# Attention with a position bias, a dense layer and top-2 experts on one core: an integer intermediate moved to PSUM, a 64-column subtraction moved to GpSimd, and another order for the last pair of experts

## The chip, the cores and the metric

The kernel runs on one core of a Trainium2 chip. The metric is the device time of one execution in microseconds, the median of three runs. The core has five engines with a queue of instructions each: TensorE (PE, and PEld for its weight loads), VectorE (DVE), ScalarE (ACT), GpSimd (POOL) and SyncE (SP), which here only issues DMAs. Every engine takes its own instructions in the order in which they stand in its queue.

## The reference

Three layers follow one another. B = 2, 8 heads, 576 positions, 64 numbers per head; 1152 rows of 512 numbers between the layers.

```python
scores = scale * q @ k^T + bias          # bias from a small MLP of |i - j|, one table per head
attn = softmax(scores)
x = (attn @ v)                           # (2, 8, 576, 64) -> (1152, 512)

h = x @ w_in                             # 512 -> 2048, weights given as float64
x = (h * sigmoid(h)) @ w_out             # 2048 -> 512

logits = x @ w_gate + log1p(exp(x @ w_noise)) * noise
top2, top2_w = ...                       # two of 8 experts for each row, softmax of their logits
for e in range(8):
    out[rows of e] += weight * (relu(x[rows of e] @ w1[e]) @ w2[e])
```

## The kernel before

**Two 16-bit parts.** TensorE multiplies float16. Every float32 operand is split into a high part, rounded to float16, and a low part, which is the rest; a product is then two or three matmuls. The split is an ACT copy to float16 and a subtraction on DVE or POOL.

**Attention** (`attention`, `att`). The 576 query rows are five chunks (four of 128 rows for each batch, one of 64 rows for both batches together), called a to e. For each chunk, head and batch there is one tile of 128 queries by 576 keys, 72 tiles in all. A tile's steps: scores on PE (lines 388 and 391), bias added and row maximum taken on DVE (431), a scalar (435), the exponential on ACT (436), its float16 copy `pr` on ACT (438), the low part of keys 0 to 511 on POOL (through the helper's line 117), and the low part of the last 64 keys on DVE (442). Then one DMA transposes `pr` (451, issued by SP), and PE multiplies by V (456, 457, 459). `xf` (467) ends four heads of a chunk.

**Bias waves** (`bias_wave`). For each chunk a table of the bias is made in 18 groups: a mask on DVE (`mk`, 337), 16 small matmuls into one PSUM tile `pb` (345, 346), one half taken out of it by DVE (359) and one by ACT (361), and their sum on POOL.

**Weight conversion** (`conv`). `w_in` and `w_out` arrive as float64 and are turned into float32 with integer operations, in 32 pieces of 128 by 512. DVE reads the high word and masks and shifts it (500), joins the sign (504) and the low word's top bits (505), all into the int32 tile `tt`, which lies in SBUF. ACT scales it in place (509) and writes the high part (510), POOL writes the low part (511). All 32 pieces go this way.

**PSUM.** Eight banks: the tag `gen` has three tiles of one bank, used in turn by `pb`, by `ph` of the dense layer and the experts, and by some smaller ones; `pq` has two tiles of two banks (scores, expert outputs), `av` one bank. A tile of a tag takes the place of the one allotted three earlier, and waits until that one has been read.

**Order.** Through the first two thirds bias waves, attention, conversion and dense layer are merged by a list of due times (`PLAN`, `merge`). A scheduler then sets the order in each engine's queue, so an edit in one place can move instructions in another.

**Experts** (`experts`). The eight experts go in four pairs g = 0 to 3, each expert with 320 slots for rows. `up(k, c0, n)` multiplies by w1 for n slots (lines 979 to 981, eight groups of 12 matmuls), with the activation on ACT (985) and the low part on DVE (986). `down(k, c0, col)` multiplies 128 slots by w2 (995 to 997, 24 matmuls). `down_last` does the remaining 64 slots of both experts together (1010). Each result is scaled on ACT (964) and added to the output by an indirect DMA that POOL issues (958); each of these waits for the one before.

```python
            yield from chain(up(0, 0, CAP), up(1, CAP, CAP))
        yield from down_last()
        if g > 0:
            yield from chain(down(0, 0, 0), down(1, 192, 1))
        yield from chain(down(0, 128, 2), down(1, 64, 3))
```

Of the kernel before, what the change touches and what calls it, by code (L numbers as in the profile page):

```python
# [23 lines left out]
CAP = 320  # L24
# [84 lines left out]
def body(ctx, tc, nc, A):  # L109
# [298 lines left out]
    def attention(c, xT):  # L408
# [3 lines left out]
        for hg in range(2):  # L412
# [5 lines left out]
            for h in range(4 * hg, 4 * hg + 4):  # L418
                bt = bias_load(c, h)
                if h % 4 == 1 and nxt is not None and nxt not in QT:  # L420
                    q_prep(*nxt)
                pqs = []
                for bi, b in enumerate(bs):
                    parts = [(0, 128, b)] if c < 4 else [(0, 64, 0), (64, 64, 1)]
                    if bi == 0 or c not in JQ:
                        qs = range(bi, nb if c in JQ else bi + 1)
                        scores(c, h, QT[c, hg], qs, pqs)
                    pq = pqs[bi]
                    z = at.tile([128, S], F32, name="z", tag="z", bufs=3)
                    st = at.tile([128, 4], F32, name="st", tag="st", bufs=4)  # L430
                    LAST["z", c, h, bi] = V.tensor_tensor_reduce(out=z, in0=pq, in1=bt, scale=1.0, scalar=NEG,  # L431
                                           op0=OP.add, op1=OP.max, accum_out=st[:, 1:2])
                    if h == 0 and c in ZX:
                        follow(LAST["z", c, h, bi], "xl")
                    V.tensor_scalar(st[:, 2:3], st[:, 1:2], -0.125, LN256, op0=OP.mult, op1=OP.add)  # L435
                    SC.activation(z, z, AF.Exp, bias=st[:, 2:3], scale=0.125, accum_out=sums[:, bi, h % 4:h % 4 + 1])  # L436
                    pr = at.tile([128, 2 * S], F16, name="pr", tag="pr", bufs=3)
                    SC.activation(pr[:, :S], z, AF.Copy)  # L438
                    if PLO:
                        V.tensor_sub(pr[:, 640:640 + PLO], z[:, :PLO], pr[:, :PLO])  # L440
                    STT(G, pr[:, 640 + PLO:1152], z[:, PLO:512], 1.0, pr[:, PLO:512])
                    V.tensor_sub(pr[:, 576:640], z[:, 512:], pr[:, 512:576])  # L442
                    pt = at.tile([128, 1152], F16, name="pt", tag="pt", bufs=3).rearrange("p (k q) -> p k q", k=9)
                    if c == ORDER[0] and h >= PTP:
                        for k0, k1 in ((0, 5), (5, 9)):
                            pp = gen("pp").bitcast(F16).rearrange("p (k q) -> p k q", q=128)
                            for k in range(k0, k1):
                                PE.transpose(pp[:, k - k0], pr[:, 128 * k:128 * k + 128], eye0)
                            SC.activation(pt[:, k0:k1], pp[:, :k1 - k0], AF.Copy)
                    else:  # L450
                        SP.dma_start_transpose(out=pt, in_=pr)
                    for p0, n, bb in parts:
                        o = av[p0:p0 + n, bi, h % 4, :]
                        for k in range(5):
                            lt = pt[:, k, p0:p0 + n]
                            mm(o, lt, VH[:, k, bb, h, :], start=(k == 0), stop=False)
                            mm(o, lt, VL[:, k, bb, h, :], start=False, stop=False)
                        for k in range(4):
                            mm(o, pt[:, 5 + k, p0:p0 + n], VH[:, k, bb, h, :], start=False, stop=(k == 3))
                    yield  # L460
# [25 lines left out]
    def conv(key, half, src):  # L486

        hi, lo = wtile(), wtile()
        WT[key, half] = (hi, lo)
        for pc in range(8):  # L490
            if pc % 3 in RG.get((key, half), ()):
                raw = m1.tile([128, 512], mybir.dt.int64, name="raw", tag="gt", bufs=NGT)
            else:
                raw = m1.tile([128, 512], mybir.dt.int64, name="raw", tag="raw", bufs=NRAW)
            with tc.issue_after(LAST[GATE].ins):
                SC.dma_start(raw, src(pc))
            v = raw.bitcast(I32).rearrange("p (n t) -> p n t", t=2)
            lw, hw = v[:, :, 0], v[:, :, 1]
            tt = m1.tile([128, 512], I32, name="tt", tag="yT", bufs=2)
            i = V.tensor_scalar(tt, hw, 0x07FFFFFF, 3, op0=OP.bitwise_and, op1=OP.logical_shift_left)  # L500
            if (key, half) in GC:
                follow(i, GC[key, half])
            LAST["tt", key, half, pc] = i
            V.scalar_tensor_tensor(tt, hw, -1073741824, tt, op0=OP.bitwise_and, op1=OP.bitwise_or)  # L504
            V.scalar_tensor_tensor(tt, lw, 29, tt, op0=OP.logical_shift_right, op1=OP.bitwise_or)  # L505
            f = tt.bitcast(F32)
            cs = slice(512 * pc, 512 * pc + 512)
            if pc in CP[key][half]:
                SC.activation(f, f, AF.Copy, scale=32.0)
                SC.activation(hi[:, cs], f, AF.Copy)  # L510
                G.tensor_sub(lo[:, cs], f, hi[:, cs])  # L511
            else:
                SC.activation(hi[:, cs], f, AF.Copy, scale=32.0)
                STT(V, lo[:, cs], f, 32.0, hi[:, cs])
            yield
# [117 lines left out]
    def chain(*gs):  # L633
        for g in gs:
            yield from g
# [331 lines left out]
    def experts(g):  # L967
# [3 lines left out]
        def up(k, c0, n):  # L971

            a_h, a_l = EW[2 * g + k, 0]
            for f in range(8):
                ph = gen("ph")[:, :n]
                for j in range(4):
                    cs = slice(1024 * j + 128 * f, 1024 * j + 128 * f + 128)
                    xh, xl = xg[:, j, c0:c0 + n], xg[:, 4 + j, c0:c0 + n]
                    mm(ph, a_h[:, cs], xh, start=(j == 0), stop=False)  # L979
                    mm(ph, a_h[:, cs], xl, start=False, stop=False)  # L980
                    mm(ph, a_l[:, cs], xh, start=False, stop=(j == 3))  # L981
                if (k, f) not in hts:
                    hts[k, f] = m2.tile([128, 2, CAP], F16, name="ht", tag="ht", bufs=20)
                ht = hts[k, f][:, :, c0 - CAP * k:c0 - CAP * k + n]
                SC.activation(ht[:, 0], ph, AF.Relu)  # L985
                V.scalar_tensor_tensor(ht[:, 1], ph, 0.0, ht[:, 0], op0=OP.max, op1=OP.subtract)  # L986
                yield
# [27 lines left out]

        if g == 0:
            yield from chain(up(0, 0, 128), up(1, 512, 128), down(0, 0, 0), down(1, 192, 1), up(0, 128, 192), up(1, 320, 192))
        else:
            yield from chain(up(0, 0, CAP), up(1, CAP, CAP))
        yield from down_last()  # L1020
# [113 lines left out]
```

## Time and profile before

| What | Value |
|---|---|
| median of 3 runs | 755.66 us (752.59 to 762.42) |
| the profiled execution, its own time | 758.37 us |
| its span in the trace | 756.6 us |
| busy over the span: PE, DVE, ACT, POOL | 606.9, 502.3, 377.9, 366.5 us |

The profile is one execution. "Busy" counts an instruction from its start to its end, with any time for which it is held up inside. "Idle before" is the time for which an engine had nothing running, put down to what it waited for. The span is the stretch from the first to the last instruction; 1.8 us of the execution lie around it.

### The profile page before, as it was taken

How to read it: one execution, taken by the hardware profiler on the slowest of the kernel's cores; microseconds unless marked ns; L12 is line 12 of the kernel's file. 1: busy time of each engine (PE TensorE's matmuls, PEld its weight loads, DVE VectorE, ACT ScalarE, POOL GpSimd, SP SyncE). 2: the span in 40 equal slices, each digit the busy share in tenths (PEclk: the TensorE clock that was granted, in tenths of full speed). 3: DMA queues.
4: the chain of work that ended last, by engine and by line, in shares of the span. 5: the costliest groups of instructions: out<-in, count | busy, mean ns of one | idle time of the engine just before them, and what ended most of it. 6: DMA issues, size and time to landing. Idle time of an engine off the chain costs nothing.

```text
span 756.6 us, 16562 instructions
## 1 busy us (share of the span) xinstructions
PE 606.9 (80%) x6371; PEld 402.6 (53%) x6371; DVE 502.3 (66%) x1093; ACT 377.9 (50%) x805; POOL 366.5 (48%) x366
## 2 busy tenths in 40 slices
PE   0565666578587878997999889979889899999992
PEld 0462344456344666565765664757665554655640
DVE  2999999999999699556952755656657642740200
ACT  2666467668644577345732644761355543541210
POOL 2686677687967687436761552303405114103022
PEclk9875557599788998998999999999999999999996
DMA  4547788778876699887996967764999959903123
GB/s 113 135 140 243 158 161 179 183 210 186 159 179 182 161 174 199 145 172 116 159 237 124 183 129 220 192 225 110 238 240 246 308 182 230 299 4 42 17 25 43
DMA packets 203143, 125.77 MB, mean 166 GB/s; under 512 B 153076, under 2 KB 175732, under 8 KB 203060
## 3 DMA queue, kind: packets, MB, share of 16 engines
q1 hardware_dynamic: 170868, 90.39, 52.2%
q10 hardware_dynamic: 27648, 24.32, 11.0%
q0 software_dynamic: 4544, 9.97, 7.1%
q8 instruction: 51, 0.84, 0.4%
q14 instruction: 32, 0.26, 0.1%
HBM read 74.83 MB, written 18.22 MB: 123 GB/s over the span
## 4 chain that ended last, share of the span: by engine, by line
PE 29%; DVE 29%; DMA 18%; issue 11%; ACT 4%; POOL 4%; SPq 3%; ACTq 1%; another core or an unknown queue 1%; DVEq 0%; POOLq 0%
DMA stg<-in_e 6%; DVE mk L337 4%; PE ph L979 3%; DVE z L431 3%; DMA pt<-pr 3%; PE ph L981 3%; DVE pr L442 3%; PE ph L980 3%; DVE tt L504 3%; DVE tt L505 3%; PE po L1010 3%; DVE tt L500 2%; PE po L996 2%; PE po L995 2%; PE po L997 2%
## 5 line engine op out<-in xcount | busy, mean ns | idle before, releaser
L117 POOL TENSOR_TENSOR pr<-z,pr 128x512 f16<-128x512 f32 x72 | 94.6, 1321 | 23.3 <-ACT pr L438 14.7
L553 PE MATMUL ph<-xT,wb 128*128 128x256 f16 (+1 forms) x320 | 84.9, 275 | 11.5 <-DVE th L558 7.1
L345 PE MATMUL pb<-rhs_h,mk 128*128 128x64 f16 (+1 forms) x720 | 66.4, 210 | 26.4 <-ACT ta L361 11.6
L337 DVE TENSOR_TENSOR mk<-io,tau 128x1024 f16<-128x1024 f16 (+1 forms) x90 | 85.8, 959 | 0.7 <-PE pb L346 0.7
L117 POOL TENSOR_TENSOR gt<-th,gt 128x256 f16<-128x256 f32 (+1 forms) x80 | 56.0, 704 | 60.6 <-ACT gt L562 58.1
L117 POOL TENSOR_TENSOR g<-ta 128x256 f32<-128x256 f32 (+1 forms) x72 | 63.6, 884 | 44.3 <-ACT ta L361 37.4
L554 PE MATMUL ph<-xT,wb 128*128 128x256 f16 (+1 forms) x320 | 84.8, 275 | 0.0
L555 PE MATMUL ph<-xT,wb 128*128 128x256 f16 (+1 forms) x320 | 84.8, 275 | 0.0
L958 POOL DMA_INDIRECT out<-ot,idx x18 | 27.6, 1536 | 114.5 <-ACT ot L964 52.5
L388 PE MATMUL pq<-km,qt 128*128 128x512 f16 (+2 forms) x160 | 51.7, 437 | 28.9 <-DVE st L431 28.4
L436 ACT ACTIVATE z<-z,st 128x576 f32<-128x576 f32 x72 | 55.3, 769 | 34.9 <-DVE st L435 34.4
L986 DVE SCALAR_TENSOR_TENSOR ht<-ph,ht 128x320 f16<-128x320 f32 (+2 forms) x80 | 32.8, 420 | 54.3 <-ACT ht L985 53.8
L345 PEld LDWEIGHTS <-mk 128*128 128x128 f16 (+1 forms) x720 | 57.8, 111 | 19.3 <-issue 7.7
L346 PEld LDWEIGHTS <-mk 128*128 128x128 f16 (+1 forms) x720 | 56.9, 112 | 20.1 <-issue 19.2
L346 PE MATMUL pb<-rhs_l,mk 128*128 128x64 f16 (+1 forms) x720 | 65.9, 209 | 0.0
L924 DVE SCALAR_TENSOR_TENSOR wb<-stg,wb 128x1024 f16<-128x1024 f32 (+1 forms) x48 | 48.3, 1042 | 23.6 <-ACT wb L923 20.2
L923 ACT ACTIVATE wb<-stg 128x1024 f16<-128x1024 f32 (+1 forms) x48 | 41.8, 908 | 33.5 <-DMA stg<-in_e 29.9
L576 PE MATMUL py<-wb,gt 128*128 128x512 f16 x144 | 56.0, 391 | 1.5 <-DVE st L431 1.3
L577 PE MATMUL py<-wb,gt 128*128 128x512 f16 x144 | 56.1, 389 | 1.1 <-POOL wb L511 1.1
L578 PE MATMUL py<-wb,gt 128*128 128x512 f16 x144 | 55.8, 388 | 0.0
L985 ACT ACTIVATE ht<-ph 128x320 f16<-128x320 f32 (+2 forms) x80 | 29.2, 378 | 50.0 <-PE ph L981 49.8
L511 POOL TENSOR_TENSOR wb<-tt,wb 128x512 f16<-128x512 f32 x32 | 43.7, 1366 | 17.3 <-ACT wb L510 17.1
(198 smaller groups left out, 1794.0 us busy)
## 6 DMA issues: line engine op xcount, KB each, us to landing
stg<-in_e SPq DMA_DIRECT2D x64, 512.0 KB
raw<-in_w_in ACTq DMA_DIRECT2D x16, 512.0 KB
raw<-in_w_out ACTq DMA_DIRECT2D x16, 512.0 KB
bt<-eb SPq DMA_DIRECT2D x24, 288.0 KB
eb<-g SPq DMA_DIRECT2D x12, 512.0 KB
yrows<-yh SPq DMA_DIRECT2D x9, 256.0 KB
out<-zero SPq DMA_DIRECT2D x3, 768.0 KB
bt<-eb SPq DMA_DIRECT2D x16, 144.0 KB
```

Of the source, the lines that this page charges most:

```text
L117: G.tensor_tensor(o, x, y, op=op)
L337: i = V.tensor_tensor(mk[:, :, :n], io16[:, None, i0:i0 + n].to_broadcast([128, 8, n]), tv, op=OP.is_gt)
L345: mm(pb[:n, :, t, :], m, rhs_h, start=True, stop=False)
L346: mm(pb[:n, :, t, :], m, rhs_l, start=False, stop=True)
L388: i = mm(pq[p0:p0 + n, :512].rearrange("p (m s) -> p m s", m=2), lt, KM[b][r0:r0 + nr, :, h].rearrange("p m x s -> p m (x s)"), start=star ...
L436: SC.activation(z, z, AF.Exp, bias=st[:, 2:3], scale=0.125, accum_out=sums[:, bi, h % 4:h % 4 + 1])
L553: mm(ph, hh[:, cs], xh, start=(j == 3), stop=False)
L554: mm(ph, hh[:, cs], xl, start=False, stop=False)
L555: mm(ph, hl[:, cs], xh, start=False, stop=(j == 0))
L576: mm(pys[i], gh, oh[:, cs], start=(f == 0), stop=False)
L577: mm(pys[i], gh, ol[:, cs], start=False, stop=False)
L578: mm(pys[i], gl, oh[:, cs], start=False, stop=(f == 15))
```

## The change

Three edits. The low part of a tile's last 64 keys is taken by POOL in place of DVE, behind the subtraction of the other 512. `tt` becomes a PSUM tile of the tag `gen`; ACT's scaling writes to a new SBUF tile `fs`, which has the place that `tt` had. The last pair of experts runs `up` of the second expert in two parts, the second part being its first 128 slots (which lie at columns 512 to 639), and its `down` steps in another order.

```diff
-                    V.tensor_sub(pr[:, 576:640], z[:, 512:], pr[:, 512:576])
+                    G.tensor_sub(pr[:, 576:640], z[:, 512:], pr[:, 512:576])
...
-            tt = m1.tile([128, 512], I32, name="tt", tag="yT", bufs=2)
+            tt = ps.tile([128, 512], I32, name="tt", tag="gen", bufs=3)
...
-                SC.activation(f, f, AF.Copy, scale=32.0)
-                SC.activation(hi[:, cs], f, AF.Copy)
-                G.tensor_sub(lo[:, cs], f, hi[:, cs])
+                fs = m1.tile([128, 512], F32, name="fs", tag="yT", bufs=2)
+                SC.activation(fs, f, AF.Copy, scale=32.0)
+                SC.activation(hi[:, cs], fs, AF.Copy)
+                G.tensor_sub(lo[:, cs], fs, hi[:, cs])
...
+        elif g == 3:
+
+            yield from chain(up(0, 0, CAP), up(1, CAP, 192), down(0, 0, 0), down(0, 128, 2), down_last(), up(1, 512, 128),
+                             down(1, 64, 3), down(1, 192, 1))
+            return
```

Below line 508 the changed kernel's line numbers are one higher than before, in `experts` too.

POOL's queue in the attention of the first chunk, before: `pr` is the low part of 512 keys, `wb<-tt` the low part of a conversion piece, `g` a bias sum.

```order
L117 TENSOR_TENSOR pr<-z,pr 128x512 x2
L511 TENSOR_TENSOR wb<-tt,wb 128x512
L117 TENSOR_TENSOR pr<-z,pr 128x512
L117 TENSOR_TENSOR g<-ta 128x8x32
L511 TENSOR_TENSOR wb<-tt,wb 128x512
```

POOL's queue at the same place, now.

```order
L117 TENSOR_TENSOR pr<-z,pr 128x512
L442 TENSOR_TENSOR pr<-z,pr 128x64
L117 TENSOR_TENSOR g<-ta 128x8x32
L512 TENSOR_TENSOR wb<-fs,wb 128x512
L117 TENSOR_TENSOR pr<-z,pr 128x512
```

Each 512-key subtraction is now followed at once by its 64-key one, so the transposing DMA waits for POOL alone.

DVE's queue where the conversion ends and the third bias wave begins, before (`z` and `st` are a tile's scores and scalars).

```order
L431 ISA z,st<-pq,bt 128x576
L431 ISA st 128x1
L504 SCALAR_TENSOR_TENSOR tt<-raw,tt 128x512
L359 TENSOR_TENSOR ta<-pb,xij 128x256
L337 TENSOR_TENSOR mk<-io_109,tau 128x1024
L442 TENSOR_TENSOR pr<-z,pr 128x64
L435 TENSOR_SCALAR st<-st 128x1
```

DVE's queue there, now (`th` is the dense layer's activation).

```order
L504 SCALAR_TENSOR_TENSOR tt<-raw,tt 128x512
L505 SCALAR_TENSOR_TENSOR tt<-raw,tt 128x512
L559 SCALAR_TENSOR_TENSOR th<-th,ph 128x256
L359 TENSOR_TENSOR ta<-pb,xij 128x256
L337 TENSOR_TENSOR mk<-io_109,tau 128x1024 x2
```

The last conversion pieces stand ahead of the third wave now instead of among its groups: 53 masks stood ahead of the last conversion step before, 39 now. By the first `xf` of the third chunk both queues hold the same 68 masks, all 32 pieces and 28 (before: 30) of the `th`.

ACT's queue from the end of the third pair to the end of the last, before (`ht` are activations of `up`, `ot` scaled results).

```order
L985 ACTIVATE ht<-ph 128x320 x3
L964 ACTIVATE ot<-po,ws 128x512 x3
L985 ACTIVATE ht<-ph 128x320 x12
L964 ACTIVATE ot<-po,ws 64x512 x2
L964 ACTIVATE ot<-po,ws 128x512 x4
```

ACT's queue in the last pair, now.

```order
L986 ACTIVATE ht<-ph 128x320 x4
L986 ACTIVATE ht<-ph 128x192 x8
L965 ACTIVATE ot<-po,ws 128x512 x2
L965 ACTIVATE ot<-po,ws 64x512 x2
L986 ACTIVATE ht<-ph 128x128 x6
L965 ACTIVATE ot<-po,ws 128x512
L986 ACTIVATE ht<-ph 128x128 x2
L965 ACTIVATE ot<-po,ws 128x512
```

Four of the six results now come ahead of the last 128 slots' activations, and two behind most or all of them.

## Rows read from the trace of the kernel before

**Rows 1.** Stretch, its length, busy us: PE, PEld, DVE, ACT, POOL; granted clock, DMA share, GB/s.
```profile
50.00:250.00 200.00, 132.98 (x1545) 88.00 (x1543) 197.21 (x344) 122.47 (x258) 149.72 (x128) 0.74 0.73 180
250.00:292.60 42.60, 37.07 (x519) 29.73 (x518) 35.05 (x87) 28.47 (x73) 32.40 (x36) 0.96 0.87 183
292.60:456.00 163.40, 143.81 (x1774) 100.17 (x1773) 99.17 (x282) 81.06 (x204) 85.75 (x107) 0.96 0.83 160
```

**Rows 2.** DVE's groups, 50 to 292.6 us: count, busy us, mean ns, idle before.
```profile
L337 DVE TENSOR_TENSOR mk<-io,tau 128x1024 f16<-128x1024 f16 x51 | 50.6, 998 | 0.0
L505 DVE SCALAR_TENSOR_TENSOR tt<-raw,tt 128x512 int32<-128x512 int32 x32 | 34.8, 1086 | 0.3
L504 DVE SCALAR_TENSOR_TENSOR tt<-raw,tt 128x512 int32<-128x512 int32 x32 | 31.5, 983 | 0.3
L442 DVE TENSOR_TENSOR pr<-z,pr 128x64 f16<-128x64 f32 x42 | 27.8, 666 | 1.4 <-ACT pr L438 1.4
L500 DVE TENSOR_SCALAR tt<-raw 128x512 int32<-128x512 int32 x32 | 22.8, 712 | 0.0
```

**Rows 3.** Timeline of DVE and POOL, 99.9 to 103.6 us: start us, duration us.
```profile
99.93 1.60 POOL L117 TENSOR_TENSOR pr<-z,pr 128x512 f16<-128x512 f32 x1
100.43 1.17 DVE L442 TENSOR_TENSOR pr<-z,pr 128x64 f16<-128x64 f32 x1
101.86 0.68 DVE L504 SCALAR_TENSOR_TENSOR tt<-raw,tt 128x512 int32<-128x512 int32 x1
101.91 1.64 POOL L511 TENSOR_TENSOR wb<-tt,wb 128x512 f16<-128x512 f32 x1 [0.39 <-ACT wb L510]
```

**Rows 4.** Single lines on DVE, whole span: count, duration ns min/median/max.
```profile
L442 DVE TENSOR_TENSOR pr<-z,pr x72: 161/638/1795, 72.1 to 445.5; 128x64 f16<-128x64 f32 x72
L504 DVE SCALAR_TENSOR_TENSOR tt<-raw,tt x32: 676/694/1661, 55.0 to 239.1; 128x512 int32<-128x512 int32 x32
L500 DVE TENSOR_SCALAR tt<-raw x32: 409/517/1396, 52.2 to 236.8; 128x512 int32<-128x512 int32 x32
L359 DVE TENSOR_TENSOR ta<-pb,xij x72: 368/412/425, 65.0 to 404.1; 128x256 f32<-128x256 f32 x54, 64x256 f32<-64x256 f32 x18
```

**Rows 5.** POOL's subtractions, line 117, whole span, as in rows 4.
```profile
L117 POOL TENSOR_TENSOR gt<-th,gt x80: 421/671/1232, 153.3 to 492.6; 128x256 f16<-128x256 f32 x64, 128x128 f16<-128x128 f32 x16
L117 POOL TENSOR_TENSOR pr<-z,pr x72: 1143/1170/1718, 71.6 to 445.6; 128x512 f16<-128x512 f32 x72
```

**Rows 6.** Waits of SP's DMA queue, 50 to 292.6 us: total us, times, longest.
```profile
SPq L451 <- DVE pr L442: 68.8, 26, 9.8
```

**Rows 7.** Timeline of one `gen` tile of a bias wave and its next user.
```profile
91.21 0.24 PE L345 MATMUL pb<-rhs_h,mk 128*128 128x64 f16 x1
...
102.05 0.39 ACT L361 ACTIVATE ta<-pb 128x256 f32<-128x256 f32 x1 [0.22 <-DVE ta L359]
...
102.49 0.21 PE L345 MATMUL pb<-rhs_h,mk 128*128 128x64 f16 x1 [3.02 <-ACT ta L361]
```

**Rows 8.** Timeline of the first conversion piece.
```profile
52.25 1.40 DVE L500 TENSOR_SCALAR tt<-raw 128x512 int32<-128x512 int32 x1
...
59.90 0.63 ACT L509 ACTIVATE tt<-tt 128x512 f32<-128x512 f32 x1
```

**Rows 9.** Timeline of the end: ACT's last result and POOL's last scatter.
```profile
742.16 0.69 ACT L964 ACTIVATE ot<-po,ws 128x512 f32<-128x512 f32 x1 [4.49 <-PEq L1053]
...
749.04 1.55 POOL L958 DMA_INDIRECT out<-ot,idx  x1 [3.96 <-DMA out<-ot,idx]
```

**Rows 10.** Timeline of PE in `up`: pairs of matmuls with 320 and 128 slots.
```profile
716.83 0.30 PE L980 MATMUL ph<-xg,ew 128*128 128x320 f16 x1
716.97 0.30 PE L981 MATMUL ph<-xg,ew 128*128 128x320 f16 x1
...
505.80 0.22 PE L979 MATMUL ph<-xg,ew 128*128 128x128 f16 x1
505.85 0.22 PE L980 MATMUL ph<-xg,ew 128*128 128x128 f16 x1
```

## The prediction

> **What bounds the kernel now.** I read the busy time by stretch first. From 50 to 250 us DVE is busy for 197.2 of 200 us, and from there to 292.6 us, where the first `xf` of the third chunk starts, for 35.05 of 42.6 [rows 1]. No other engine comes near: POOL has 149.7 and PE 133.0 of the 200, and PE is granted only 0.74 of its clock there. DVE is the wall of this stage (50 to 292.6 us, 242.6 us, DVE busy 232.3 of them).
>
> The groups of that stage came next. DVE spends 89.1 us on the three integer steps (32 each) and 27.8 us on 42 subtractions of 64 columns [rows 2]. That the second sum is absurd is the clue: 64 columns take 0.666 us on average, as much as 512 columns at their fastest (0.676). The same instruction varies from 0.161 to 1.795 us, the second step from 0.676 to 1.661 [rows 4]. The timeline shows why: the subtraction that starts at 100.43 ends at 101.60, just behind POOL's, which ran from 99.93 to 101.53; then DVE's step at 101.86 runs at its fastest, and POOL's instruction of 101.91 takes 1.64 us [rows 3] where the fastest of that size is 1.143 [rows 5]. One of the two engines is held until the other is done, and the held time is counted as busy. Line 359, of whose two inputs one lies in PSUM, is never held: 0.368 to 0.425 us in 72 executions [rows 4]. So I read the holding as a matter of instructions whose inputs both lie in SBUF (and of the first step, which runs above one column a nanosecond when free).
>
> **The change part by part.**
>
> *Subtraction to POOL.* It takes 42 instructions off DVE in the stage: 27.8 us [rows 2]. On POOL no subtraction of 64 columns is to be seen. Its fastest with 128 and with 512 columns take 0.421 and 1.143 us [rows 5], 1.88 ns a column; the line through both gives 0.301 us at 64. The bounds are DVE's own 0.161 and the 0.421 of twice the width; I take 0.30, so POOL gets 42 x 0.30 = 12.6 us more in the stage (6.8 to 17.7). Behind it in POOL's queue stand the bias sums and the conversion's low parts, whose readers come 0.3 us later each. What hides that is POOL's idle time, 60 of 242.6 us; without it, 12.6 us would be paid. SP's transposes waited 68.8 us, in 26 waits, for the DVE instruction [rows 6]; now they wait for POOL, which does both parts in one go, so a tile's chain gets rather shorter. After the stage 30 more leave DVE, which is busy for only 99.2 of 163.4 us there, while PE is busy for 143.8 [rows 1]: I take nothing for them; with every one on the path, 30 x 0.30 = 9.0 us would be lost.
>
> *Integer steps in PSUM.* Each then has one SBUF input, as line 359 has. The second and third steps should run at 0.69 us, the median of the one that is held least [rows 4]. The first runs at 0.409 us when it is not held, faster per column than the others, so it may lose that speed with its output in PSUM; DVE writing to PSUM is nowhere in this trace. The bounds for all 96 steps: 32 x (0.409 + 2 x 0.676) = 56.4 us if all keep their fastest time, 89.1 us (no gain) if PSUM costs what the waiting did. I take 96 x 0.69 = 66.2 us, nearest to the rows of single steps: 22.9 us off DVE.
>
> The Trainium skill, "VectorE: DVE Perf Modes", section "Why PSUM operands drop a tier", says that a PSUM operand rules out the mode in which DVE uses both SBUF ports, which speaks against this edit. With it the first step costs 0.69 (as I took); without it, 0.41 and 9.0 us less over the 32. No row here shows which.
>
> The price is a wait. `tt` now takes its turn among three `gen` tiles, so the first step waits until ACT has emptied the tile allotted three before, and every mask, score and bias step behind it in DVE's queue waits with it; PE's next `pb` or `ph` waits in turn for line 509's reading. This is the rival below.
>
> *DVE's sum.* 232.3 - 27.8 - 22.9 = 181.6 us of work remain up to the first `xf` of the third chunk, by which both orders hold the same masks and pieces. How long the stage then lasts is a choice of pace. At the pace of a wall, 232.3/242.6 = 0.957, it lasts 189.8 us and 52.8 us are gained; but nothing else then waits, and it would. I take the pace of the stretch just behind the wall, where bias, attention and dense layer also share the engines, 35.05/42.6 = 0.823 [rows 1]: 181.6/0.823 = 220.7 us, a gain of 21.9 us. POOL would have 182.1 + 12.6 = 194.7 us in it, 0.88, if none of its own held time went. The later stages keep their length and start earlier.
>
> *Last pair.* Before, the last result is ready at 742.16 + 0.69 = 742.85, yet its scatter starts at 749.04, since each scatter waits for the transfer of the one before; one step of that chain is 3.96 + 1.55 = 5.51 us [rows 9]. One `down` takes 4.49 + 0.69 = 5.18 us by ACT's row, so the six scatters, started late, never catch up. In the new order four results come before the last 128 slots' `up`. Between the last two results PE has 24 matmuls of 128 slots and 24 of `down`: 24 x 0.05 + 5.18 = 6.4 us, more than 5.51, so the last scatter should start when its result is ready, up to 6.2 us earlier. Splitting 320 slots in 192 and 128 adds 96 matmuls: 0.14 us for 320, 0.05 for 128 [rows 10], some 0.08 between them for 192, so 0.13 against 0.14 and no loss to be seen; I allow 0.7 us. Gain 5.5 us (bounds 0 and 6.2).
>
> *Sum.* 21.9 + 5.5 = 27.4 us. The profiled execution took 758.37 us with what lies around its span; 758.4 - 27.4 = **731.0 us**. It is 2.7 us above the median of the runs shown and inside their spread, and I let that stand.
>
> **The rivals.**
>
> *The held time moves.* Masks still have two SBUF inputs: 51 of them, 0.998 us each [rows 2]. If they meet whatever the others met, DVE only loses the unheld work: 42 x 0.161 = 6.8 us off and 66.2 - 56.4 = 9.8 us on, nothing gained in the stage. Only the end remains: 758.4 - 5.5 = 752.9 us. For it: POOL gets more to do, not less. Against: of the instructions that can be held, the masks stay and 138 (42 and 96) go.
>
> *The PSUM tiles become the bound, slower than before.* One `pb` began at 91.21; the next user of its place, three tiles on, began at 102.49, right behind ACT's reading, after PE had idled 3.02 us for it [rows 7]. That is 11.2 us in one place. The first conversion piece needed its tile from 52.25 to 60.53, 8.3 us [rows 8]. In the stage 51 `pb` and 28 `ph` take turns; 32 `tt` make it 111. Three places give each 3 x 242.6 / 111 = 6.56 us before the stage gets longer than it was. At 7 us it lasts 259 us: +16.4 - 5.5 = +10.9, **769.3 us**. At 6.56 us and over this decides. For it: both rows are above. Against: a `pb` stayed so long because DVE was behind with its work, which the change eases; four instructions (3 x 0.69 + 0.63 = 2.7 us) are all that a `tt` needs.
>
> **How the numbers follow.** My forecast has 0.62 (own range 712 to 748: from a pace of 0.90, 40.8 us, with the full 6.2 us at the end, to one of 0.78, 9.8 us, with none of it), the moved time 0.27, the PSUM tiles 0.11. A measurement of this kernel can tell about 2% (15 us) from no change, so the border is 740.5 us. Of the forecast's 0.62, 0.56 lies below it and 0.06 above; the second case lies within 2%; of the third, 0.09 is slower and 0.02 within. Faster 0.56, same 0.35, slower 0.09. The range 712 to 758 takes in the second case with 5 us for the spread of its runs, and leaves out most of the third and the forecast's ends.
>
> **What would show it.** Right: steps 504 and 505 at 0.68 to 0.75 us with hardly a spread; DVE busy for clearly under 0.957 of the first 242 us; the third chunk's first `xf` near 270 us; the last scatter within 1 us of its result. The held time moved: masks well over 1.0 us and DVE still at 0.95. The PSUM tiles: DVE idle before line 500 and PE idle before `pb` and `ph`, released by ACT, and DVE no longer busy though the stage is no shorter. Wrong altogether: PSUM steps over 0.9 us each, or a 64-column subtraction on POOL over 0.42 us.

## The result, and the profile after

The changed kernel took 739.85 us (median of 5 executions, 731.07 to 743.17) beside 757.8 us for the kernel before, a ratio of 0.973 with the interval 0.968 to 0.978. Run a second time among other executions of before it took 739.17 us (ratio 0.974, 0.969 to 0.980). The forecast was 731.0 us with a range of 712 to 758. That range takes in the time of the kernel before as well, so that the measurement lies in it says little; the terms of the sum have to be looked at one by one. The profiled execution is the longest of its five (743.17 us, span 741.4), so against the profile of before (758.37 us) it is only 15.2 us shorter.

First the busy time by stretch of the changed kernel, with the second border at its own first `xf` of the third chunk (columns as in [rows 1]).

```profile
50.00:250.00 200.00, 135.15 (x1594) 92.26 (x1594) 151.14 (x318) 123.61 (x264) 142.22 (x162) 0.74 0.83 191
250.00:285.30 35.30, 29.76 (x428) 23.22 (x427) 27.11 (x69) 24.69 (x63) 29.78 (x39) 0.95 0.68 159
50.00:285.30 235.30, 164.91 (x2020) 115.49 (x2020) 178.25 (x386) 148.30 (x327) 172.00 (x200) 0.78 0.81 186
285.30:450.10 164.80, 147.33 (x1821) 102.07 (x1820) 82.83 (x254) 81.91 (x207) 96.73 (x142) 0.97 0.80 160
```

DVE has 178.25 us of work in the stage, where before it had 232.3. Yet the stage takes 235.3 us in place of 242.6. Of 54 us taken off DVE, 7.3 have come off the stage. The other 46.7 are added to DVE's idle time, which is 57 us now and was 10.3.

Next the single lines, in the form of [rows 4, 5]; the lines of `pr` are POOL's.

```profile
L504 DVE SCALAR_TENSOR_TENSOR tt<-raw,tt x32: 677/688/697, 55.1 to 212.8; 128x512 int32<-128x512 int32 x32
L500 DVE TENSOR_SCALAR tt<-raw x32: 673/690/696, 53.6 to 211.9; 128x512 int32<-128x512 int32 x32
L117 POOL TENSOR_TENSOR pr<-z,pr x72: 1147/1158/1616, 69.7 to 441.4; 128x512 f16<-128x512 f32 x72
L442 POOL TENSOR_TENSOR pr<-z,pr x72: 297/307/793, 70.8 to 442.5; 128x64 f16<-128x64 f32 x72
```

A step with its intermediate in PSUM varies by 20 ns (the first step by 23), where line 504 varied from 676 to 1661; the first step has lost its fast 409 ns. POOL's 64 columns take 0.297 us when nothing holds them.

DVE's groups in the stage follow, as in [rows 2], and then DVE's waits there (what it waited for: us in total, times, longest).

```profile
L337 DVE TENSOR_TENSOR mk<-io,tau 128x1024 f16<-128x1024 f16 x51 | 48.0, 952 | 0.2 <-PE pb L346 0.2
L504 DVE SCALAR_TENSOR_TENSOR tt<-raw,tt 128x512 int32<-128x512 int32 x32 | 22.0, 687 | 0.1
L500 DVE TENSOR_SCALAR tt<-raw 128x512 int32<-128x512 int32 x32 | 21.9, 688 | 15.3 <-DMA raw<-in_w_out 11.8 <-DMA raw<-in_w_in 2.4 <-ACT fs L510 0.7
L505 DVE SCALAR_TENSOR_TENSOR tt<-raw,tt 128x512 int32<-128x512 int32 x32 | 21.9, 688 | 0.2
```

```profile
DVE tt L500 <- DMA raw<-in_w_out: 11.8, 7, 3.1
DVE th L559 <- ACT th L558: 11.2, 8, 3.4
DVE z L431 <- DMA bt<-eb: 6.9, 2, 6.0
DVE ta L359 <- PE pb L346: 6.7, 7, 2.5
DVE z L431 <- POOL pr L442: 4.8, 6, 2.0
DVE ta L359 <- DMA xij<-in_xij: 3.7, 1, 3.7
```

No single wait has taken the place of the old wall: DVE now waits for loads of weights, for ACT's half of the dense layer, for the bias table, for PE. `ACT fs`, which would be the PSUM tiles of the rival, is 0.7 us. The six waits shown and `ACT fs` are some 46 of the 57 us.

The end, answering to [rows 9]: ACT's last result and POOL's last scatter.

```profile
733.07 0.69 ACT L965 ACTIVATE ot<-po,ws 128x512 f32<-128x512 f32 x1 [4.09 <-PEq L1059]
...
734.03 1.57 POOL L959 DMA_INDIRECT out<-ot,idx  x1 [4.85 <-ACT ot L965]
```

The scatter now starts 0.27 us behind the end of its result; before, it was 6.2 us behind. So profile against profile, 7.3 us come from the stage, 5.9 from the wait of the last scatter, and 2.0 remain for everything else. One trace of each is a coarse measure: a second trace of the changed kernel, below, divides its gain otherwise.

### The profile page after: what moved, and what is told of

It is laid out like the page before. It is cut to its first block, busy times and chain, and to the rows that moved or that the text cites. A ratio compares the mean times of both kernels' runs of the same rounds, so it can differ in the third digit from the quotient of the medians.

```text
span 741.4 us, 16711 instructions
## 1 busy us (share of the span) xinstructions
PE 603.6 (81%) x6467; PEld 405.8 (55%) x6467; DVE 433.7 (58%) x1029; ACT 378.0 (51%) x813; POOL 369.4 (50%) x438
## 4 chain that ended last, share of the span: by engine, by line
PE 36%; DMA 28%; DVE 14%; issue 7%; ACT 6%; POOL 4%; SPq 2%; ACTq 0%; POOLq 0%; DVEq 0%
DMA pt<-pr 8%; DMA stg<-in_e 6%; PE ph L980 3%; PE ph L982 3%; PE ph L981 3%; DVE mk L337 3%; PE po L1011 2%; DMA raw<-in_w_out 2%; DMA bt<-eb 2%; DMA gx<-yrows,idx 2%; PE po L998 2%; PE po L996 2%; PE po L997 2%; DVE z L431 2%; PE ph L554 2%
## 5 line engine op out<-in xcount | busy, mean ns | idle before, releaser
L117 POOL TENSOR_TENSOR pr<-z,pr 128x512 f16<-128x512 f32 x72 | 86.6, 1203 | 37.8 <-ACT pr L438 28.7
L554 PE MATMUL ph<-xT,wb 128*128 128x256 f16 (+1 forms) x320 | 85.9, 278 | 9.4 <-DVE th L559 4.6
L555 PE MATMUL ph<-xT,wb 128*128 128x256 f16 (+1 forms) x320 | 85.8, 278 | 0.0
L556 PE MATMUL ph<-xT,wb 128*128 128x256 f16 (+1 forms) x320 | 85.7, 278 | 0.0
L959 POOL DMA_INDIRECT out<-ot,idx x18 | 27.4, 1525 | 108.4 <-ACT ot L965 68.9
L345 PE MATMUL pb<-rhs_h,mk 128*128 128x64 f16 (+1 forms) x720 | 63.4, 208 | 19.0 <-ACT ta L361 7.2
L117 POOL TENSOR_TENSOR g<-ta 128x256 f32<-128x256 f32 (+1 forms) x72 | 59.1, 821 | 38.5 <-ACT ta L361 38.5
L117 POOL TENSOR_TENSOR gt<-th,gt 128x256 f16<-128x256 f32 (+1 forms) x80 | 53.1, 667 | 49.6 <-ACT gt L563 49.3
L388 PE MATMUL pq<-km,qt 128*128 128x512 f16 (+2 forms) x160 | 50.6, 429 | 23.7 <-DVE st L431 23.4
L346 PEld LDWEIGHTS <-mk 128*128 128x128 f16 (+1 forms) x720 | 55.4, 110 | 16.4 <-issue 15.6
L345 PEld LDWEIGHTS <-mk 128*128 128x128 f16 (+1 forms) x720 | 56.2, 110 | 13.4 <-issue 6.5
L456 PE MATMUL av<-vh,pt 128*128 128x64 f16 (+1 forms) x400 | 38.8, 206 | 28.8 <-DMA pt<-pr 27.4
L431 DVE CUSTOM_DVE_ANT_0 z<-pq,bt 128x576 f32<-128x576 f32 x56 | 41.6, 751 | 31.9 <-DMA bt<-eb 17.6
L438 ACT ACTIVATE pr<-z 128x576 f16<-128x576 f32 x72 | 48.1, 675 | 16.8 <-DMA pt<-pr 16.5
L980 PE MATMUL ph<-xg,ew 128*128 128x128 f16 (+2 forms) x224 | 50.8, 246 | 5.8 <-DVE ht L987 4.0
```

The lines of the kernel that those rows point to most:

```text
L117: G.tensor_tensor(o, x, y, op=op)
L345: mm(pb[:n, :, t, :], m, rhs_h, start=True, stop=False)
L346: mm(pb[:n, :, t, :], m, rhs_l, start=False, stop=True)
L388: i = mm(pq[p0:p0 + n, :512].rearrange("p (m s) -> p m s", m=2), lt, KM[b][r0:r0 + nr, :, h].rearrange("p m x s -> p m (x s)"), start=star ...
L554: mm(ph, hh[:, cs], xh, start=(j == 3), stop=False)
L555: mm(ph, hh[:, cs], xl, start=False, stop=False)
```

## The experiments

Each kernel was timed beside the kernel before on the same chip; "before" is 755.97 us in the first group of four, 754.74 in the second and 757.32 in the third. An edit also lets the scheduler set another order in the queues, which no experiment here could keep fixed; a difference of a few us between two kernels can be that.

**The last pair alone** (the changed kernel's `elif g == 3` added to the kernel before).

```diff
+        elif g == 3:
+            yield from chain(up(0, 0, CAP), up(1, CAP, 192), ..., down(1, 64, 3), down(1, 192, 1))
+            return
```

> Only the new order of the last pair, all else as before; the queues up to the last pair stand as before. Every theory: the last scatter starts within 0.5 us of its result instead of 6.2 us behind it, and the time falls by 5 to 6 us (ratio 0.992 to 0.994). If the gain of the end were lost to the 96 added matmuls, it would be under 3 us.

749.69 us, ratio 0.992 (0.989 to 0.995): 6.3 us. The last scatter starts at 739.30, its result ends at 738.34 + 0.69:

```profile
738.34 0.69 ACT L964 ACTIVATE ot<-po,ws 128x512 f32<-128x512 f32 x1 [3.89 <-PEq L1058]
...
739.30 1.57 POOL L958 DMA_INDIRECT out<-ot,idx  x1 [4.95 <-ACT ot L964]
```

The term of the last pair stands as worked out.

**The subtraction alone.**

```diff
-                    V.tensor_sub(pr[:, 576:640], z[:, 512:], pr[:, 512:576])
+                    G.tensor_sub(pr[:, 576:640], z[:, 512:], pr[:, 512:576])
```

> Only the 64-column subtraction on GpSimd. Theory 1 (the held time goes for good, and the stage is bound by DVE as long as its queue is full): DVE busy up to the first xf of the third chunk falls by 25 to 30 us, masks and integer steps keep their mean (about 1.0 us each), the first xf of the third chunk comes 6 to 12 us earlier and the total falls by 4 to 10 us. Theory 2 (the held time moves to the masks and integer steps): their means rise to 1.1 us or more, and the total falls by under 3 us.

758.47 us, ratio 1.005 (1.001 to 1.008): nothing gained, rather 2.5 us lost. Its groups of DVE and POOL from 50 to 250 us:

```profile
L500 DVE TENSOR_SCALAR tt<-raw 128x512 int32<-128x512 int32 x32 | 24.0, 749 | 7.4 <-POOL wb L511 4.5 <-DMA raw<-in_w_out 2.8
L504 DVE SCALAR_TENSOR_TENSOR tt<-raw,tt 128x512 int32<-128x512 int32 x32 | 33.1, 1036 | 0.4
L117 POOL TENSOR_TENSOR pr<-z,pr 128x512 f16<-128x512 f32 x32 | 46.1, 1440 | 6.6 <-issue 5.6 <-ACT pr L438 0.9
L442 POOL TENSOR_TENSOR pr<-z,pr 128x64 f16<-128x64 f32 x32 | 19.5, 610 | 0.0
```

With the integer steps still in SBUF, 64 columns on POOL take 0.610 us, twice their free time; DVE's second step is held longer than before (1036 against 983 ns, [rows 2]); and a new wait stands ahead of the first step, for POOL's conversion part. Up to the first `xf` of the third chunk (291.4 us) DVE is busy for 212.8 us, 19.5 less than before, and POOL for 201.3, 19.2 more, where the prediction gave POOL 12.6 more. The stage is 1.2 us shorter. What leaves DVE comes back on POOL.

**The intermediate in PSUM alone.**

```diff
-            tt = m1.tile([128, 512], I32, name="tt", tag="yT", bufs=2)
+            tt = ps.tile([128, 512], I32, name="tt", tag="gen", bufs=3)
...
+                fs = m1.tile([128, 512], F32, name="fs", tag="yT", bufs=2)
...
```

> Only the integer intermediate in PSUM. Theory 1: the 96 steps take 0.69 us each, line 442 keeps its 0.63 us since it is held by GpSimd as before, the total falls by 3 to 8 us. Theory 2 (the held time moves): line 442 and the masks rise by a fifth or more, the total falls by under 3 us. Theory 3 (the order: with the steps in PSUM the scheduler puts the third bias wave behind the conversion, 39 masks ahead of its last step against 53): the gain up to the last integer step is 15 us or more and is given back by the start of the third chunk's attention, which comes less than 5 us earlier.

758.4 us, ratio 1.002 (0.999 to 1.006): nothing gained. The last integer step ended 25.7 us earlier than before in the profile (217.2 against 242.9), but the first `xf` of the third chunk began at 289.9 against 292.6. DVE's and POOL's subtractions from 50 to 250 us, and the wait of SP's transposes from 50 to 292.6 us:

```profile
L442 DVE TENSOR_TENSOR pr<-z,pr 128x64 f16<-128x64 f32 x32 | 16.0, 502 | 1.7 <-ACT pr L438 1.4
L117 POOL TENSOR_TENSOR pr<-z,pr 128x512 f16<-128x512 f32 x32 | 37.3, 1173 | 23.5 <-ACT pr L438 20.7 <-issue 1.1 <-POOL pr L117 1.0
```

```profile
SPq L451 <- DVE pr L442: 46.0, 21, 7.7
```

POOL is nearly free of its held time (1173 ns in place of 1414), but the transposes still wait for a DVE instruction that is held behind POOL and queued behind steps and masks: 46.0 us, where before it was 68.8 [rows 6]. DVE is busy for 196.4 of the 239.9 us, 35.9 us less than before, and the stage is 2.7 us shorter: here too DVE's time has turned into idle time. The traced execution took 764.97 us, 6.6 more than the median, so its places in time are rough.

**Both, without the last pair.** The changed kernel without its `elif g == 3`.

> Both edits of the conversion and attention stage, without the last pair's order. Theory 1 (the two edits need each other: with one alone VectorE still ends the stage late or its chain is broken elsewhere, with both the gain of the stage reaches the end): 742 to 747 us, 9 to 13 faster than before, so that the last pair's 6 us bring it to the changed kernel's time; TensorE spends some 130 to 140 us at the lower clock, as in the changed kernel, against about 160 in the kernels with one of the two edits. Theory 2 (the parts add: +2.5 for the subtraction, +2.4 for the intermediate): 758 to 763 us, and the changed kernel's gain comes from something in the last pair that one edit alone did not show. Both kernels should give the last integer step before 220 us.

743.32 us, ratio 0.986 (0.980 to 0.991): 11.4 us. The parts do not add: +2.5 and +2.4 alone, -11.4 together; with the last pair's 6.3 us this makes 17.7, where the changed kernel beside it is 15.6 us faster than before. From 50 to 250 us, and SP's wait from 50 to 292.6 us:

```profile
L117 POOL TENSOR_TENSOR pr<-z,pr 128x512 f16<-128x512 f32 x32 | 38.4, 1200 | 14.0 <-ACT pr L438 10.0 <-issue 2.3 <-POOL pr L442 1.2
L442 POOL TENSOR_TENSOR pr<-z,pr 128x64 f16<-128x64 f32 x32 | 12.1, 377 | 0.0
```

```profile
SPq L451 <- POOL pr L442: 17.9, 13, 2.9
```

POOL does the subtraction in 0.377 us in place of 0.610, and the transposes wait 17.9 us for it in place of 46.0 for DVE. That fits a reading in which each edit takes away what kept the other from paying: the subtraction on POOL alone is held by the steps in SBUF, and with the steps in PSUM alone the transposes still wait for DVE. That both are needed is shown by the times; the way by which it reaches the end is argued only. Added up over all that they waited for, up to each kernel's first `xf` of the third chunk, SP's transposes waited 107.2 us before, 94.8 and 92.9 with one edit and 82.6 with both (88.0 in the changed kernel), so that no large wait is gone.

A rival stays beside it. With one edit the granted clock is lower than in the kernel before beside it: 0.894 and 0.896 on average over twelve executions each, against 0.903; with both it is 0.899 against 0.902, in the changed kernel's eleven 0.907. A clock lower by 0.0096 would cost up to 7 us of 757 if TensorE were on the path throughout (an estimate, worked out from these averages). So a part of what one edit alone gained can have been lost to the clock. The expectation of 130 to 140 us at the lower clock did not hold: a mean of 0.899 is some 150 of 742 us at half the clock.

**The changed kernel again.**

> The changed kernel again, among the same runs of before, for a second trace and a tighter ratio. Expected 734 to 743 us, ratio 0.968 to 0.982. Theory clock (the time at the lower clock of TensorE is what differs between executions of one kernel): the executions with the longer spans have the lower mean granted clock, 0.902 against 0.917 for 12 us, and half of the time at the lower clock is about the difference. Rival (the executions differ by transfers): span and clock are unrelated.

739.17 us, ratio 0.974 (0.969 to 0.980). Span and clock go together only in part: its longest execution (span 747.5) has the lowest clock, 0.896, but its shortest (729.6) has 0.904 and two of 737.4 have 0.909 and 0.912. In its trace the third chunk's first `xf` begins at 283.4 us, the last result of the dense layer (`yh`) at 491.4, and the end is 250.8 us behind that; in the first trace it was 285.3, 495.9 and 245.5 (before: 292.6, 502.0 and 254.6). So two executions of one kernel differ by 2 to 5 us in each of these.

**The third bias wave due earlier.** In the changed kernel, so that 53 masks stand ahead of the last integer step as before, and not 39.

```diff
-        ... "bc": (153.3, 0.38), ...
+        ... "bc": (120, 0.38), ...
```

> The changed kernel with one number of the list of due times altered, the third bias wave due at 120 instead of 153.3; 53 masks then stand ahead of the last integer step, as before the change, instead of 39. Theory 3 (the third wave came late and the third chunk's attention waited for its table): the first scores of the third chunk come 5 us or more earlier than in the changed kernel (252.0 us), and the total falls by 4 to 10 us below the changed kernel's. Theory 4 (from 215 us on TensorE's own work is the bound, whatever DVE does): the first scores may come earlier, but the second output of the third chunk (316.6 us) moves by less than 2 us, and the total stays within 3 us of the changed kernel's.

748.8 us, ratio 0.988 (0.983 to 0.993), some 9 us slower than the changed kernel. The first scores of the third chunk came at 251.7 us, no earlier than in the changed kernel (252.0), so theory 3 does not hold. The `yh` at 316.6 us, of which theory 4 speaks, is in truth the first of the second chunk; it came at 306.7 us, so theory 4 does not hold either. At the last `yh` the trace was level with the changed kernel's first (496.2 against 495.9 us), and it took 253.7 us from there, against 245.5 and 250.8 in the changed kernel's two traces, with the same code. So the other place of the wave did not cost the changed kernel its gain. Why this kernel is slower was not followed further.

**The subtraction on POOL for the first two chunks alone, or for the last three alone.** Both in the changed kernel.

```diff
-                    G.tensor_sub(pr[:, 576:640], z[:, 512:], pr[:, 512:576])
+                    (G if c in ORDER[:2] else V).tensor_sub(pr[:, 576:640], z[:, 512:], pr[:, 512:576])
```

> The subtraction of the last 64 keys is on GpSimd for the first two chunks of queries alone, and on VectorE again for the last three, where VectorE has no conversion to do. Theory 1 (in the later chunks GpSimd's subtraction stands ahead of the transposes and the next tile's softmax input waits for it, 4 to 6 us between 215 and 320 us): 3 to 6 us faster than the changed kernel, third chunk's first finished tile at 281 to 283 us. Rival (from 300 us on TensorE is full in both kernels, so that what is late before it does not matter): within 2 us of the changed kernel, the yh of the third chunk at 316 to 318 us as before.

744.46 us, ratio 0.987 (0.982 to 0.992), 5.3 us slower than the changed kernel in the same group, and the intervals lie apart. Theory 1, by which POOL's part in the late chunks is a burden, is wrong in the total, and so is the rival: having it on POOL is worth about 5 us. In the trace the third chunk's first `xf` does come early, at 277.4 us, and the `yh` of which the rival speaks (the second chunk's again) at 309.5, but from the first of these to the last `xf` it takes 170.4 us at a granted clock of 0.93, where the other twelve traces take 160.0 to 166.5 at 0.95 to 0.97, those with all subtractions on DVE among them. What the stage gained is lost there; why was not shown.

```diff
-                    G.tensor_sub(pr[:, 576:640], z[:, 512:], pr[:, 512:576])
+                    (V if c in ORDER[:2] else G).tensor_sub(pr[:, 576:640], z[:, 512:], pr[:, 512:576])
```

> The counterpart of the kernel with the first two chunks' subtraction alone on GpSimd: here the last three chunks' alone are. If the two halves of the edit add up (the whole edit is worth 13 us beside the intermediate in PSUM, of which the first two chunks' half gave 8 and the last three's 5 us): 746 to 749 us, 7 to 9 slower than the changed kernel. Rival (the late half is all that counts, since in the stage of the conversion VectorE idles anyway): within 3 us of the changed kernel, 737 to 742 us. Rival (each half is worth the whole, what counts is another order by the scheduler): 743 to 745 us.

753.61 us, ratio 0.998 (0.994 to 1.002): slower than any of the three expectations. With the first two chunks' subtraction back on DVE, all but 3.7 us of the change is gone, and SP's transposes wait for DVE again:

```profile
SPq L451 <- DVE pr L442: 31.9, 15, 7.0
```

The kernel is where the intermediate in PSUM alone (2.4 us lost) and the last pair alone (6.3 us gained) would put it together, 3.9 us below before; measured are 3.7. So beside the PSUM intermediate the late half gives nothing without the early one, and about 5 us with it: the two halves do not add either. That the wait shown is the cause is not: in this trace the third chunk's first `xf` begins at 282.05 us and the last `yh` at 494.2, as early as in the changed kernel. The traced execution took 747.9 us, though, 5.7 less than the median.

**One integer step less.** The line of the third step is left out, so the weights lose their last three bits; in the changed kernel and in the kernel before.

```diff
-            V.scalar_tensor_tensor(tt, lw, 29, tt, op0=OP.logical_shift_right, op1=OP.bitwise_or)
```

> The changed kernel without the third integer step of each conversion piece (the weights' last three bits are left out): 32 x 0.69 = 22 us less on VectorE, nothing less on any other engine. Theory 1 (VectorE still paces the stage, although it idles 40 us in it): first finished tile of the third chunk 5 to 10 us earlier and 5 to 10 us faster than the changed kernel, 730 to 734 us. Theory 2 (the stage now ends with loads, the third bias wave's handoffs and TensorE): within 3 us of the changed kernel, the idle time of VectorE up to the end of the third wave grows by about what is taken out.

733.63 us, ratio 0.969 (0.964 to 0.973), by the medians 5 to 6 us faster than the changed kernel, by the ratios some 4; the intervals overlap, so this gain is not clear of the noise. From 50 us to its first `xf` of the third chunk:

```profile
50.00:271.10 221.10, 163.33 (x2061) 115.54 (x2061) 168.03 (x358) 148.55 (x333) 174.19 (x206) 0.83 0.85 198
```

DVE is busy for 168.03 of 221.1 us, 0.760; in the changed kernel it is 178.25 of 235.3, 0.758. Of the 21.9 us that the step took there, DVE's busy time fell by 10.2 only; a part came back in other instructions (masks 1005 ns on average against 952). The stage is 14.2 us shorter than in the first trace of the changed kernel, at the same pace. This is what a stage paced by chains through DVE would do, though DVE idles a quarter of it. It is not shown by this alone: in the kernel with the first two chunks' subtraction alone on POOL, DVE had more to do than in the changed kernel (181.8 us), and the stage was shorter all the same (227.4 us).

> The kernel before without the third integer step (the weights' last three bits are left out): 34.8 us less on VectorE by the profile of before, with the time that the step was held. Theory 1 (in the kernel before VectorE's work is worth its share of the stage at the end): 10 to 20 us faster than before. Theory 2 (as with the subtraction alone, what is taken off VectorE comes back as GpSimd's held work, as waits and as TensorE's lower clock): within 4 us of before, and VectorE's masks and remaining steps as long as before or longer on average.

755.31 us, ratio 0.998 (0.995 to 1.001): 34.8 us of DVE's counted time were taken out, and at most 0.5% came off the kernel. From 50 to 250 us:

```profile
L504 DVE SCALAR_TENSOR_TENSOR tt<-raw,tt 128x512 int32<-128x512 int32 x32 | 32.8, 1029 | 0.3
L500 DVE TENSOR_SCALAR tt<-raw 128x512 int32<-128x512 int32 x32 | 26.4, 827 | 7.6 <-POOL wb L510 2.9 <-POOL gt L117 2.4 <-DMA raw<-in_w_out 2.0
L442 DVE TENSOR_TENSOR pr<-z,pr 128x64 f16<-128x64 f32 x32 | 23.7, 740 | 0.0
```

And up to its first `xf` of the third chunk, columns as in [rows 1]:

```profile
50.00:284.50 234.50, 166.04 (x2020) 115.19 (x2019) 200.95 (x391) 147.41 (x323) 168.46 (x159) 0.77 0.81 188
```

The remaining steps and the subtraction each became longer than in [rows 2] (983, 712 and 666 ns), some 8 us in the stage, and DVE waits for POOL. The masks became shorter (in the stage 952 ns against 998), so that part of theory 2 did not hold. Most of what was taken out did not come back as held time: DVE is busy for 200.95 us, where it was 232.3, and idles for 33.5, where it was 10.3. In the trace the stage is 8.1 us shorter, the last `yh` 6.2 us earlier (495.8 us), and 3.5 us of that are lost again behind it. So neither theory accounts for the whole; what is shown is that 34.8 us of counted time were worth about 2 us at the end, and 4 at the most.

**TensorE kept busy where it waits for the last token tile.** In the changed kernel, 56 transposes whose results are overwritten.

```diff
+                for r in range(56):
+                    PE.transpose(pT[:, r % 8], eye, eye)
```

> 56 transposes of the identity, with a result that is overwritten, are put ahead of the last token tile's transposes, where TensorE idles 3.3 us at 492.6 to 495.9 us and then runs the experts' first matmuls at the lower clock for 3.4 us. Theory clock (the wait costs itself and a stretch at the lower clock behind it): granted clock 1.00 through 492 to 512 us, the first expert results 1 to 2 us earlier relative to the last yh, 1 to 3 us faster than the changed kernel. Rival 1 (the stretch behind it waits for handoffs and loads in any case): within 1 us. Rival 2 (the transposes delay the work behind them, 56 by 0.053 us is 3.0 us): 1 to 3 us slower.

741.09 us, ratio 0.982 (0.977 to 0.988), 1.9 us slower than the changed kernel in the same group, with intervals that overlap. First PE in the changed kernel, then the stretches of the kernel with the transposes (columns as in [rows 1]):

```profile
495.95 0.40 PE L605 MATMUL pT<-eye__7343,yh 128*128 128x128 f16 x4 [3.32 <-ACT yh L598]
...
496.41 0.22 PE L981 MATMUL ph<-xg,ew 128*128 128x128 f16 x1
496.46 0.22 PE L982 MATMUL ph<-xg,ew 128*128 128x128 f16 x1
...
496.58 0.31 PE L981 MATMUL ph<-xg,ew 128*128 128x128 f16 x1
496.69 0.31 PE L982 MATMUL ph<-xg,ew 128*128 128x128 f16 x1
```

```profile
485.00:489.00 4.00, 4.00 (x60) 3.41 (x59) 2.66 (x5) 3.43 (x6) 0.00 (x0) 1.00 0.94 319
489.00:493.00 4.00, 2.33 (x38) 1.90 (x34) 0.69 (x1) 3.06 (x4) 0.00 (x0) 1.00 0.75 270
493.00:497.00 4.00, 3.29 (x50) 3.17 (x51) 2.19 (x11) 2.02 (x7) 0.00 (x0) 0.80 0.02 8
497.00:501.00 4.00, 4.00 (x58) 4.00 (x57) 2.32 (x14) 1.39 (x5) 0.00 (x0) 0.77 0.02 4
```

In the changed kernel PE idles 3.32 us, and behind that its matmuls of 128 columns start every 0.11 us in place of every 0.05: the lower of its two levels (1.2 and 2.4 GHz); the granted clock is 0.57 from 496 to 500 us. With the gap filled, PE still idles in smaller pieces from 489 to 497 us, and the clock falls all the same (0.80, 0.77). Of the full clock, 0.43 x 4 = 1.7 us are lost in the one kernel and (0.20 + 0.23) x 4 = 1.7 us in the other. So the stretch at the lower clock moved and did not go, and no gain shows. The sign is that of rival 2, but 1.9 us are within the noise.

## Why the prediction was right, and which term was mis-sized

- *The holding between DVE and POOL*: right. Free of it, a step takes 0.688 us. That POOL suffers as much was read correctly from [rows 3] but not put into the sum: its 512-key subtraction went from 1414 to 1226 ns on average in 50 to 250 us, and POOL is busy for 172.0 of 235.3 us (0.73) where 0.88 was worked out. The Trainium skill, "SBUF — State Buffer", section "Who interferes with whom", says that a DVE instruction contends with a reading GpSimd one when both its inputs lie in SBUF, and that one with at most one input there, outside the modes that use two ports, does not. The traces agree: 0.610 us with the steps in SBUF, 0.377 with them in PSUM, for the same instruction on POOL. Before, the first step was held with its single input too, 409 to 1396 ns [rows 4]; at its shortest it took more than one column a nanosecond.
- *Subtraction on POOL, 0.30 us*: right as the free time (0.297 to 0.307).
- *"After the stage 30 more leave DVE: I take nothing for them"*: too little. The kernel that leaves the last three chunks' 40 tiles on DVE, ten of them in the stage, is 5.3 us slower; its trace loses time between the stage and the last `xf`. Which wait carries this was not shown.
- *Integer steps, 96 x 0.69 = 66.2 us*: measured 65.8. The first step did lose its fast mode, 690 against 409 ns at the least held. By the Trainium skill's "VectorE: DVE Perf Modes", section "Why PSUM operands drop a tier", which the prediction weighed, this was to come, and the trace agrees. The page gives the reason for an operand that is read; here it is the output alone that lies in PSUM.
- *DVE's sum, 181.6 us*: measured 178.25. It took off two group sums from a busy time. Consecutive instructions of DVE overlap a little, which the busy time counts once and the groups twice (before, all groups of the stage add up to some 260 us beside the 232.3), and other instructions than the two groups became shorter as well (masks 48.0 us, before 50.6), which the sum did not have. That 54.0 us came off where 50.7 were taken off is near in part by luck. The sum also took the two edits as two savings that stand by themselves; alone, neither was worth anything at the end.
- *Pace 0.823, a stage of 220.7 us, 21.9 us gained*: this is the term that was mis-sized. In the profile the pace was 0.758, the stage 235.3 us, the gain 7.3 us. Over the four traces of kernels with both edits (changed kernel twice, without the last pair, with the filled gap) the pace was 0.758 to 0.780 and the gain 7.3 to 12.6, 10.1 on average; by the medians the two edits together are worth 11.4 us. That is half of the term. The pace was taken from the stretch behind the wall, which has no conversion in it. The waits that only the conversion has, 14.2 us for its loads and 0.7 for `fs`, make up a quarter of the 57 us of idle time; the rest is waits of kinds that occur behind the wall too, and why there are more of them was not shown.
- *The later stages keep their length*: nearly. From the stage to the last `yh` the profile is 1.2 us longer than before, and the experts, without the wait of the last scatter, are 3.2 us shorter; the second trace differs from the first by as much.
- *Last pair, 5.5 us*: right; 5.9 in the profile, 6.3 alone.
- *The held time moves*: not in the changed kernel (masks 952 ns against 998). It does move, in part, when the subtraction alone goes to POOL (masks 1047 ns in the stage, and POOL's 19.2 us) and when a step is left out. As a rival to the whole change it was wrong.
- *The PSUM tiles*: wrong. DVE waited 0.7 us for `fs`, and PE 8.0 us in the stage for tiles that `fs` had to free, while its wait of `pb` for `ta` fell from 11.6 to 5.3 us.

The sum was 27.4 us; the profiles show 15.2 and the medians 15.6 (second group) to 18.0 us (first). The mechanism, the holding and its end, was right, and so was the term of the last pair. The forecast of the time was some 8 us too low, and the wide range took that in.

## What to carry to other kernels

When two engines hold each other, the counted time of either is not a price: 34.8 us of DVE's counted time gave about 2 us in the kernel before. Make the edits that end the holding together before judging any one of them, and test parts in pairs. When a wall goes, the idle time that comes in its place has to be estimated as well: take the pace from a stretch with the same chains (the loads and handoffs of that work), not from the nearest quiet one, and give it a wide range. And do not divide a gain of 15 us among stages from one trace when two traces of one kernel differ by 2 to 5 us in each stage.

## What was not expected of the hardware

- The same 64-column subtraction on GpSimd takes 0.610 us or 0.377 us on average, by where VectorE's unrelated integer steps keep their intermediate.
- An int32 step of 512 columns on VectorE with its intermediate in PSUM takes 673 to 697 ns in all 64 executions of lines 500 and 504, under a GpSimd that is busy for 0.73 of the time.
- TensorE's granted clock can fall in a stretch that the profile counts as wholly busy: in the changed kernel to 0.70 from 512 to 516 us, behind two stretches of 4 us at full clock, busy throughout.

```profile
504.00:508.00 4.00, 4.00 (x75) 4.00 (x73) 3.65 (x29) 1.87 (x7) 0.00 (x0) 1.00 0.02 4
508.00:512.00 4.00, 4.00 (x100) 3.88 (x97) 3.25 (x21) 1.39 (x5) 1.97 (x8) 1.00 0.00 0
512.00:516.00 4.00, 4.00 (x59) 2.27 (x56) 3.10 (x14) 0.00 (x0) 2.89 (x2) 0.70 0.27 75
```

Just before it fell, PE was at 66 matmuls of 2 and 3 columns (511.36 to 513.43 us, the last 45 shown); the first matmuls of 512 columns behind them begin 0.22 us apart and, from 513.80 us on, 0.43.

```profile
512.06 1.37 PE L828 MATMUL pw<-room,oht 128*64 128x3 f16 x45
513.29 0.38 PE L996 MATMUL po<-wb,ht 128*128 128x512 f16 x1
513.51 0.50 PE L997 MATMUL po<-wb,ht 128*128 128x512 f16 x1
513.80 0.63 PE L998 MATMUL po<-wb,ht 128*128 128x512 f16 x1
514.23 0.63 PE L996 MATMUL po<-wb,ht 128*128 128x512 f16 x1
```

Whether these small matmuls brought the clock down was not tested.
